# Output stores of a fused attention and feed-forward kernel: one transfer per chunk, or four of 32 rows

## The chip, the cores and the metric

The kernel runs on one core of a Trainium2 chip. The metric is the device time of one execution in microseconds; the kernel before takes 314.96 us (median of 3 runs, 313.32 to 315.15).

## What is computed

A Nystrom attention with 32 landmarks over 8 batches of 8 heads, 576 positions of width 64, and behind it a feed-forward layer with SiLU (512 to 2048 to 512) over all 4608 tokens:

```python
q_lm = q.reshape(B, H, m, S // m, D).mean(axis=3)     # m = 32, S // m = 18
k_lm = k.reshape(B, H, m, S // m, D).mean(axis=3)
A, Bm, C = sm(q, k_lm), sm(q_lm, k_lm), sm(q_lm, k)   # softmaxes
Z = Bm.transpose(0, 1, 3, 2) / (norm1 * norminf)
for _ in range(6):
    Z = 2 * Z - Z @ Bm @ Z
attn = A @ Z @ C @ v
h = x @ w_in                                          # x: attn as (4608, 512)
out = (h * sigmoid(h)) @ w_out                        # float32, (4608, 512)
```

## The kernel before

Work goes batch by batch (b = 0 to 7). A batch has three parts: attention (`attn(b)`), the first layer (`layer1(b)`: 16 blocks of 128 of the hidden width, `h` matmuls into PSUM, SiLU on ScalarE into `gm` and `gx`), and the second layer (`layer2_batch(b)`: four chunks of 128 tokens, in every odd batch a fifth for the rest of two batches; each chunk is 16 matmuls by `w_out_sb` in four pieces of four, a copy from PSUM to `ost`, and a store to the output). `ost` is a ring of 3 buffers. There are 36 chunks, so 36 stores of 256 KB.

The 576 positions of a batch are 32 groups l of 18 positions j, and the output row of a token is 18 l + j. A chunk's 128 rows are four values of j with 32 l each; its store (L881) is one transfer with the shape 4 x 32 x 512. The fifth chunk has rows (batch, l, j) with two values of j, and its store (L887) has the shape 64 x 2 x 512.

From batch 2 on, q, k and `ce` are transposed by DMA: four transposes give `qT` (L479), two give `ct` (L717), all issued by SyncE (SP), as are all stores. The loads of q, k and v come from GpSimd's queue (L368, L375). GpSimd also adds up the landmark means in a tree of six steps for k and six for q (L516), which ends in `lm`. Loads and transposes take turns: `ct` of batch b waits for the v loads of batch b+1, the `qT` transposes of batch b+1 wait for `ct` of batch b, and the loads of batch b+2 wait for the `qT` transposes of batch b+1.

TensorE needs `lm` for the landmark scores (through `lmT`, then `sb`), `qT` for `A` and `C`, and `ct` for the product with v (`cv`). After `cv` come `zt`, `m` and the first layer.

The order of work on each engine is fixed before the program is built. The class `Plan` simulates the engines with a cost for each operation (its time on the engine, a lag until others see its result, for some a time on a shared DMA line, `dma=`) and hands out the free operation of the highest priority. The instructions are then written in that order. The costs are numbers in the source; a change of a cost changes the order on all engines, and each engine works strictly in its order.

Of the kernel before, what the change touches and what calls it, by code (L numbers as in the profile page):

```python
# [254 lines left out]
def kernel(  # L255
# [9 lines left out]
    nc = tc.nc  # L265
# [11 lines left out]
    sc = 1.0 / float(Dh) ** 0.5  # L277
    SW = 128 + L
    NPE = 2
    XLAG = 0.7  # L280

    constp = ctx.enter_context(tc.tile_pool(name="constp", bufs=1))
    natp = ctx.enter_context(tc.tile_pool(name="natp", bufs=1))
# [6 lines left out]
    def bank(o, i=0):  # L290
        return banks[o.slot[i]]
# [142 lines left out]
    def attn(b):  # L434
# [12 lines left out]
        if on_pe:  # L447
            blocks = {}
            me["qk_read"] = []
            for t in (1, 0):  # L450
                todo = [(g, jp) for g in range(NG) for jp in range(JP)]
                for i in range(0, 18, 4):
                    part = todo[i:i + 4]

                    def tmm(e, t=t, part=part, key=(t, i)):
                        ps = bank(blocks[key])
                        for n, (g, jp) in enumerate(part):
                            mm(ps[:, n * 128:(n + 1) * 128],
                               qk[:, t, g, 2 * jp:2 * jp + 2, :].rearrange("p j d -> p (j d)"),
                               idb)  # L460
                    o = blocks[t, i] = A(f"tr{t}{i}.{b}", [("PE", mm_us(128, len(part)))], tmm,
                                         [qk_ops[b, t], cid], p0 + 7 + (1 - t) * 0.5, psum=1)
                    me["qk_read"].append(o)

                    def tcp(e, t=t, i=i, n=len(part), key=(t, i)):
                        copy(e, qT[:, t].rearrange("p g j x -> p (g j) x")[:, i:i + n, :],
                             bank(blocks[key])[:, 0:n * 128].rearrange("p (n x) -> p n x", x=128))
                    c = A(f"trc{t}{i}.{b}", either(128 * len(part)), tcp, [o], p0 + 8).reads(o)
                    for g, _ in part:
                        qt_ops.setdefault((t, g), []).append(c)  # L470
        else:
            me["qk_read"] = []
            me["xts"] = []
            gate = v_ops[b][-1:] if b == NPE else prev["cts"]
            for t in (1, 0):
                for g in range(NG):
                    qt_ops[t, g] = [A(
                        f"xt{t}{g}.{b}", [("SP", 0.1)],
                        lambda e, t=t, g=g: nc.sync.dma_start_transpose(  # L479
                            out=qT[:, t, g], in_=qk[:, t, g].rearrange("p j d -> p (j d)")),  # L480
                        [qk_ops[b, t]] + use + gate, p0 + 5, dma=1.42, lag=XLAG)]
                    qt_ops[t, g][0].after = gate
                    me["qk_read"] += qt_ops[t, g]
                    me["xts"] += qt_ops[t, g]
# [191 lines left out]
        for g in range(NG):  # L676
# [36 lines left out]
                            bank(me["ctm", g, i0])[:, 0:384]), [o, prev.get("cv")],  # L713
                        p0 + 20).reads(o))
            else:
                ct_ops[g] = [A(f"ct{g}.{b}", [("SP", 0.1)], lambda e, ce=ce, ct=ct:
                               nc.sync.dma_start_transpose(  # L717
                                   out=ct, in_=ce.rearrange("p i x -> p (i x)")),
                               xs + [prev.get("cv")] + v_ops.get(b + 1, [])[-1:], p0 + 20, dma=1.42, lag=XLAG)]
                ct_ops[g][0].after = v_ops.get(b + 1, [])[-1:]  # L720
                me["cts"] += ct_ops[g]

# [66 lines left out]
    def layer1(b):  # L789
# [5 lines left out]
        for dc in range(NDC):  # L795
# [19 lines left out]
            if dc % 8 == 7:  # L815
# [3 lines left out]
                def xm(e, d0=d0, cell=cell):  # L819
                    ps = bank(cell["o"]).rearrange("p (c x) -> p c x", c=8)  # L820
                    for d in range(8):
# [10 lines left out]
                gx_ops[b].append(A(  # L832
                    f"gx{d0}.{b}", [("ACT", act_us(512))],
                    lambda e, d0=d0, cell=cell, c=c: nc.scalar.activation(  # L834
                        out=gx[:, d0:d0 + 8, c:c + 64].rearrange("p d (l j) -> p d j l", j=2),
                        in_=bank(cell["o"]).rearrange("p (d j l) -> p d j l", d=8, j=2),
                        func=AF.Silu),
                    [o], p + 0.5, table="silu").reads(o))
                gx_ops[b][-1].unit = b
        l1_done[b] = A(f"l1done.{b}", [("SP", 0.0)], lambda e: None, pes, 0.0, lag=0.0)  # L840
# [5 lines left out]
    def layer2(src, deps, prio, stores, split=False):  # L846
# [3 lines left out]
        for qt in range(4):  # L850
# [8 lines left out]
            if qt == 0:  # L859
# [5 lines left out]
        ost = ost_r[i]  # L865
        c = A(f"oc@{prio}", either(512), lambda e: copy(e, ost, bank(head[0])),
              [prev_piece, ost_st.get(i)], 900.0 + prio / 100).reads(head[0])
        st = A(f"os@{prio}", [("SP", 0.15)], lambda e: stores(ost), [c], prio, dma=0.65, lag=1.6)
        ost_st[i] = st
        return pieces  # L870

    def rows(b, n):
        return out[b * S:(b + n) * S, :].rearrange("(b l j) n -> b j l n", b=n, j=J)

    def layer2_batch(b):
        l2_last["m", b] = []
        for c in range(4):
            j0 = 8 * (c % 2) + c // 2

            def stores(ost, j0=j0):  # L880
                return nc.sync.dma_start(out=rows(b, 1)[0, j0:j0 + 7:2], in_=ost)  # L881
            l2_last["m", b] += layer2(
                lambda dc, c=c: gm_r[b % 3][:, dc, c * 128:(c + 1) * 128], lambda qt: gm_ops[b][4 * qt:4 * qt + 4],
                5000.0 + 100 * b + 10 * c, stores)
        if b % 2 == 1:
            def stores(ost):
                return nc.sync.dma_start(  # L887
                    out=out[(b - 1) * S:(b + 1) * S, :].rearrange(
                        "(b l j) n -> b l j n", b=2, j=J)[:, :, J - 2:J].rearrange(
                            "b l j n -> b l (j n)"), in_=ost)  # L890
            l2_last["x", b // 2] = layer2(
                lambda dc: gx_r[(b // 2) % 2][:, dc, :], 
                lambda qt: [gx_ops[b - 1][qt // 2], gx_ops[b][qt // 2]],
# [16 lines left out]
    with tc.manual_schedule(engines={ET.PE, ET.Activation, ET.DVE, ET.Pool, ET.SP}):  # L910
        table = None
        for o, e, t, end, switch in order:
# [2 lines left out]
                    act_func_set_id=EXP_SET, name=nc.get_next_instruction_name(),  # L915
                    engine=ET.Activation))
            r = o.emit(e)
            if o.dma:
                o.ins = r.ins
            for x in o.after:  # L920
                tc.add_manual_dep(o.ins, x.ins.name, mybir.DependencyInfo(
                    mybir.DependencyClass.Sync, mybir.DependencyReason.DATA),
# [34 lines left out]
```

## Time and profile before

| | |
|---|---|
| time, median of 3 runs | 314.96 us |
| time of the profiled execution | 314.78 us |
| its span, first to last instruction | 313.0 us |
| mean granted TensorE clock | 0.937 of 2.4 GHz |
| TensorE matmul busy | 269.5 us (86%) |
| ScalarE busy | 179.7 us (57%) |
| GpSimd busy | 106.9 us (34%) |
| VectorE busy | 96.6 us (31%) |
| queue of GpSimd's loads | 18.35 MB, 35.3% of 16 DMA engines |
| queue of SP's stores and transposes | 18.88 MB, 29.6% of 16 DMA engines |

Busy shares are means over the span. A transfer counts on the DMA engines by the time that its packets took. SP does no computing; a row "SPq" is the time that SP took to issue a transfer, not the time that it needed to land.

### The profile page before, as it was taken

What the parts mean: (1) busy time and instruction counts of PE and PEld (TensorE: products, weight loads), DVE (VectorE), ACT (ScalarE), POOL (GpSimd) and SP (SyncE); (2) the same over time, 40 slices, a digit from 0 to 9 for tenths busy, and PEclk for the clock granted to TensorE, in tenths of its full rate; (3) what the DMA queues carried; (4) which work ended last, traced back from release to release, by engine and by line L of the source; (5) the groups of instructions that cost most, each with busy time, mean ns of one, the idle gap of its engine ahead of it and who ended that gap; (6) DMA issues with size and microseconds to landing.
All of it is one profiled execution on the core that took longest, in us unless ns stands there. A gap on an engine that the chain in (4) does not pass through costs nothing.

```text
span 313.0 us, 5933 instructions
## 1 busy us (share of the span) xinstructions
PE 269.5 (86%) x2367; PEld 135.0 (43%) x2367; DVE 96.6 (31%) x258; ACT 179.7 (57%) x405; POOL 106.9 (34%) x133
## 2 busy tenths in 40 slices
PE   7998999939889638998799249997999999999991
PEld 5965545414344214453444024444445544444440
DVE  1676028400555611405346114035365300000000
ACT  1776986448826914898149209985369975112110
POOL 8157319453924590485041931295000000000000
PEclk9999999968999956999799659999999999999998
DMA  6999997969386928696669257866951011132222
GB/s 113 209 197 201 206 209 129 163 136 169 60 135 123 206 66 178 116 154 69 129 132 199 68 71 139 165 98 106 193 95 44 17 31 37 40 96 64 75 68 97
DMA packets 58076, 37.60 MB, mean 120 GB/s; under 512 B 39105, under 2 KB 49345, under 8 KB 58049
## 3 DMA queue, kind: packets, MB, share of 16 engines
q0 software_dynamic: 15232, 18.35, 35.3%
q1 hardware_dynamic: 42816, 18.88, 29.6%
q8 instruction: 18, 0.29, 0.4%
q14 instruction: 10, 0.07, 0.1%
HBM read 36.70 MB, written 9.44 MB: 147 GB/s over the span
## 4 chain that ended last, share of the span: by engine, by line
PE 52%; DMA 29%; ACT 6%; POOL 4%; SPq 3%; issue 2%; DVE 2%; POOLq 0%; ACTq 0%
PE ps L323 52%; DMA v<-in_v_dram 11%; DMA ct<-ce 7%; DMA w_in_sb<-in_moe_w_in_dram 7%; SPq L479 3%; ACT gm L811 3%; DMA qT<-qk 3%; POOL qk L368 2%; POOL v L375 2%; ACT gx L834 1%; ACT L914 1%; DVE bbd L576 1%; ACT ce L691 0%; DVE bm L570 0%; POOL lm L516 0%
## 5 line engine op out<-in xcount | busy, mean ns | idle before, releaser
L323 PE MATMUL ps<-w_out_sb,gm 128*128 128x512 bf16 x512 | 122.1, 382 | 0.0
L811 ACT ACTIVATE gm<-ps 128x512 bf16<-128x512 f32 x128 | 67.4, 642 | 30.6 <-PE ps L323 30.4
L323 PE MATMUL ps<-etn,m 128*128 128x64 bf16 (+1 forms) x512 | 75.5, 299 | 0.1
L323 PEld LDWEIGHTS <-gm 128*128 128x128 bf16 x512 | 47.4, 98 | 52.7 <-issue 2.9
L323 PEld LDWEIGHTS <-m 128*128 128x128 bf16 x512 | 33.1, 101 | 30.1 <-issue 7.1
L333 ACT COPY ost<-ps 128x512 f32<-128x512 f32 x25 | 14.7, 587 | 50.8 <-PE ps L323 50.7
L516 POOL TENSOR_TENSOR sa<-qk 128x576 f32<-128x576 bf16 x24 | 31.0, 1311 | 34.4 <-DMA qk<-in_k_dram 33.9
L620 DVE SCALAR_TENSOR_TENSOR st<-st,ps 128x320 bf16<-128x320 bf16 (+3 forms) x54 | 21.6, 408 | 46.0 <-PE ps L323 42.8
L323 PE MATMUL ps<-v,ct 96*64 96x128 bf16 x192 | 10.0, 251 | 15.6 <-DMA ct<-ce 14.7
L368 POOL DMA_DIRECT2D qk<-in_k_dram x8 | 6.0, 745 | 51.2 <-DMA qT<-qk 50.0
L335 DVE CAST m<-ps 128x512 bf16<-128x512 f32 x31 | 19.8, 686 | 9.0 <-PE ps L323 9.0
L516 POOL TENSOR_TENSOR sb<-sa 128x512 f32<-128x512 f32 (+1 forms) x24 | 21.6, 901 | 1.8
L333 ACT CAST m<-ps 128x512 bf16<-128x512 f32 x33 | 17.9, 617 | 3.0 <-PE ps L323 2.9
L323 PE MATMUL ps<-idb,lm 128*128 128x128 bf16 x32 | 4.7, 240 | 16.5 <-POOL lm L516 16.5
L335 DVE COPY ost<-ps 128x512 f32<-128x512 f32 x11 | 7.6, 689 | 32.7 <-PE ps L323 32.7
L375 POOL DMA_DIRECT2D v<-in_v_dram x24 | 13.9, 589 | 6.1 <-DMA w_out_sb<-in_moe_w_out_dram 3.7
L323 PE MATMUL ps<-w_out_sb,gx 128*128 128x512 bf16 x64 | 15.9, 379 | 0.0
L323 PEld LDWEIGHTS <-ct 96*64 96x64 bf16 x192 | 7.1, 126 | 20.3 <-DMA ct<-ce 17.2
L323 PE MATMUL ps<-zer 128*128 128x256 bf16 x95 | 14.5, 295 | 1.1 <-DVE zer L402 1.1
L323 PE MATMUL ps<-st 128*128 128x160 bf16 (+1 forms) x96 | 15.2, 234 | 0.0
L691 ACT ACTIVATE ce<-ps 128x288 bf16<-128x288 f32 x32 | 12.7, 412 | 3.9 <-PE ps L323 3.9
L323 PEld LDWEIGHTS <-st 128*128 128x128 bf16 x96 | 9.3, 103 | 12.3 <-issue 3.7
(68 smaller groups left out, 260.7 us busy)
## 6 DMA issues: line engine op xcount, KB each, us to landing
out_dram<-ost SPq DMA_DIRECT2D x36, 256.0 KB
qk<-in_k_dram POOLq DMA_DIRECT2D x8, 576.0 KB, 9.4
qk<-in_q_dram POOLq DMA_DIRECT2D x8, 576.0 KB, 12.3
v<-in_v_dram POOLq DMA_DIRECT2D x24, 192.0 KB, 13.3
w_out_sb<-in_moe_w_out_dram POOLq DMA_DIRECT2D x4, 512.0 KB, 10.8
w_in_sb<-in_moe_w_in_dram POOLq DMA_DIRECT2D x4, 256.0 KB, 9.6
w_in_sb<-in_moe_w_in_dram POOLq DMA_DIRECT2D x8, 128.0 KB, 7.4
qT<-qk SPq DMA_TRANSPOSE x24
```

Source lines behind the costliest of these rows:

```text
L323: nc.tensor.matmul(out=out_ap, lhsT=lhsT, rhs=rhs, start=start, stop=stop, skip_group_check=True)
L333: nc.scalar.copy(out=out, in_=in_)
L335: nc.vector.tensor_copy(out=out, in_=in_)
L368: lambda e, t=t, src=src: nc.gpsimd.dma_start(out=qk_r[b % 2][:, t].rearrange("p g j d -> p g (j d)"), in_=src[b].rearrange("(g h) (l j) d ...
L375: lambda e, a=a: nc.gpsimd.dma_start(out=v_r[b % 2][a * L:(a + 1) * L, :, :], in_=v[b].rearrange("h (l a x) d -> a l h (x d)", l=L, a=VA)[ ...
L479: lambda e, t=t, g=g: nc.sync.dma_start_transpose(out=qT[:, t, g], in_=qk[:, t, g].rearrange("p j d -> p (j d)")),
L516: lambda e: nc.gpsimd.tensor_tensor(out=o_, in0=a_, in1=b_, op=OP.add),
L576: bbd_op = chain("bbd", 0.2, lambda: nc.vector.tensor_tensor(out=bbd, in0=bc(bmt, 4, 2), in1=bc(hmask, NG, 1), op=OP.mult), [bmt_op, prev. ...
L620: nc.vector.scalar_tensor_tensor(out=s2[:, g0:g1, lo:SW], in0=s[:, g0:g1, lo:SW], scalar=2.0, in1=ps[:, 0:NG * SW].rearrange("p (g x) -> p ...
L691: nc.scalar.activation(out=ce[:, :, 0:VP].rearrange("p (i c) (a l) -> p c a i l", c=2, a=VA)[:, c], in_=bank(me[f"C{g}"], c)[:, 0:HS].rear ...
L811: lambda e, dc=dc, cell=cell: nc.scalar.activation(out=gm[:, dc, :], in_=bank(cell["o"]), func=AF.Silu),
L834: lambda e, d0=d0, cell=cell, c=c: nc.scalar.activation(out=gx[:, d0:d0 + 8, c:c + 64].rearrange("p d (l j) -> p d j l", j=2), in_=bank(ce ...
```

## The change

Each store of a chunk is issued as four transfers, one for each j (32 rows of 512 numbers, 64 KB). For the fifth chunk to be cut in this way its rows must lie as (batch, j, l), so the SiLU of `gx` writes them as they come from PSUM and no longer interleaved. The planner's costs change too: a transpose takes 1.38 of SP (before 0.1, and 1.42 of the DMA line), a chunk's store 2.2 of SP (before 0.15, and 0.65 of the DMA line), the lag of a transpose is 1.9 (before 0.7), that of a store 1.9 (before 1.6). The last piece of the diff only keeps the instruction for the manual dependencies of operations that have no `dma` any more.

```diff
-    XLAG = 0.7
+    XLAG = 1.9
...
-                        f"xt{t}{g}.{b}", [("SP", 0.1)],
+                        f"xt{t}{g}.{b}", [("SP", 1.38)],
...
-                        [qk_ops[b, t]] + use + gate, p0 + 5, dma=1.42, lag=XLAG)]
+                        [qk_ops[b, t]] + use + gate, p0 + 5, lag=XLAG)]
...
-                ct_ops[g] = [A(f"ct{g}.{b}", [("SP", 0.1)], lambda e, ce=ce, ct=ct:
+                ct_ops[g] = [A(f"ct{g}.{b}", [("SP", 1.38)], lambda e, ce=ce, ct=ct:
...
-                               xs + [prev.get("cv")] + v_ops.get(b + 1, [])[-1:], p0 + 20, dma=1.42, lag=XLAG)]
+                               xs + [prev.get("cv")] + v_ops.get(b + 1, [])[-1:], p0 + 20, lag=XLAG)]
...
-                        out=gx[:, d0:d0 + 8, c:c + 64].rearrange("p d (l j) -> p d j l", j=2),
-                        in_=bank(cell["o"]).rearrange("p (d j l) -> p d j l", d=8, j=2),
-                        func=AF.Silu),
+                        out=gx[:, d0:d0 + 8, c:c + 64],
+                        in_=bank(cell["o"]).rearrange("p (c x) -> p c x", c=8), func=AF.Silu),
...
-        st = A(f"os@{prio}", [("SP", 0.15)], lambda e: stores(ost), [c], prio, dma=0.65, lag=1.6)
+        st = A(f"os@{prio}", [("SP", 2.2)], lambda e: stores(ost), [c], prio, lag=1.9)
...
-    def rows(b, n):
-        return out[b * S:(b + n) * S, :].rearrange("(b l j) n -> b j l n", b=n, j=J)
+    def store_js(b, js, ost, p0):
+        for i, j in enumerate(js):
+            nc.sync.dma_start(out=out[b * S:(b + 1) * S, :].rearrange("(l j) n -> j l n", j=J)[j],
+                              in_=ost[p0 + L * i:p0 + L * i + L, :])
...
-                return nc.sync.dma_start(out=rows(b, 1)[0, j0:j0 + 7:2], in_=ost)
+                store_js(b, range(j0, j0 + 7, 2), ost, 0)
...
-                return nc.sync.dma_start(
-                    out=out[(b - 1) * S:(b + 1) * S, :].rearrange(
-                        "(b l j) n -> b l j n", b=2, j=J)[:, :, J - 2:J].rearrange(
-                            "b l j n -> b l (j n)"), in_=ost)
+                for bb in range(2):
+                    store_js(b - 1 + bb, (J - 2, J - 1), ost, 64 * bb)
```

The order on GpSimd differs at one place, in batch 2: the end of the tree for `lm_88` (its steps into `sb_87` and `lm_88`) and the loads of batch 3 into `qk_81` and `v_85`. Minus is before, plus the changed kernel:

```order
 L516 TENSOR_TENSOR sa_86<-sb_87 128x2x128
+L516 TENSOR_TENSOR sb_87<-sa_86 128x2x64
+L516 TENSOR_TENSOR lm_88<-sb_87,sa_86 128x256
 L368 DMA qk_81<-in_k_dram 128x2x1152
 L368 DMA qk_81<-in_q_dram 128x2x1152
 L375 DMA v_85<-in_v_dram 32x8x384 x3
-L516 TENSOR_TENSOR sb_87<-sa_86 128x2x64
-L516 TENSOR_TENSOR lm_88<-sb_87,sa_86 128x256
 L516 TENSOR_TENSOR sa_86<-qk_81 128x576 x2
```

The two tree steps have moved ahead of the five loads. On SP, these are the transfers from the `qT` transposes of batch 3 (into `qT_83`) to the `ct` transposes of batch 4 in the kernel before:

```order
L479 DMA_TRANSPOSE qT_83<-qk_81 128x9x128 x4
L881 DMA out_dram<-ost_125 4x32x512
L881 DMA out_dram<-ost_123 4x32x512
L881 DMA out_dram<-ost_124 4x32x512
L717 DMA_TRANSPOSE ct_110<-ce_108 128x6x128
L717 DMA_TRANSPOSE ct_111<-ce_109 128x6x128
L887 DMA out_dram<-ost_125 64x2x512
L479 DMA_TRANSPOSE qT_82<-qk_80 128x9x128 x4
L881 DMA out_dram<-ost_123 4x32x512
L717 DMA_TRANSPOSE ct_110<-ce_108 128x6x128
```

and the same stretch in the changed kernel:

```order
L479 DMA_TRANSPOSE qT_83<-qk_81 128x9x128 x4
L873 DMA out_dram<-ost_125 32x512 x4
L873 DMA out_dram<-ost_123 32x512 x4
L873 DMA out_dram<-ost_124 32x512 x4
L873 DMA out_dram<-ost_125 32x512 x4
L717 DMA_TRANSPOSE ct_110<-ce_108 128x6x128
L717 DMA_TRANSPOSE ct_111<-ce_109 128x6x128
L479 DMA_TRANSPOSE qT_82<-qk_80 128x9x128 x4
L873 DMA out_dram<-ost_123 32x512 x4
L717 DMA_TRANSPOSE ct_110<-ce_108 128x6x128
```

Each store is four rows, and the store of the fifth chunk stands before the `ct` transposes of batch 3 and no longer behind them. Between the `qT` and the `ct` transposes of batches 2 to 6 there were 2, 3, 1, 4 and 2 stores, and there are 2, 4, 1, 4 and 2 now. On TensorE the order is the same up to batch 2 and differs from there on in where the second layer's pieces stand.

## Rows read from the trace of the kernel before

**Rows 1.** The chain that ended last, by engine, shares of the span (page).
```profile
PE 52%; DMA 29%; ACT 6%; POOL 4%; SPq 3%; issue 2%; DVE 2%; POOLq 0%; ACTq 0%
```

**Rows 2.** Windows: stretch, us; busy (count) PE PEld DVE ACT POOL; clock, DMA share, GB/s.
```profile
60.00:244.00 184.00, 150.96 (x1411) 70.77 (x1407) 66.78 (x174) 116.49 (x268) 75.08 (x87) 0.90 0.69 125
184.00:192.00 8.00, 7.90 (x72) 4.15 (x73) 1.84 (x7) 4.44 (x9) 0.00 (x0) 0.72 0.89 145
246.00:306.00 60.00, 60.00 (x321) 27.80 (x319) 1.30 (x3) 21.18 (x40) 0.00 (x0) 1.00 0.19 54
```

**Rows 3.** Timeline of TensorE: start, us, instruction, [idle before <-what ended it].
```profile
68.88 0.39 PE L323 MATMUL ps<-idb,lm 128*128 128x128 bf16 x2 [5.37 <-POOL lm L516]
...
111.75 0.40 PE L323 MATMUL ps<-idb,lm 128*128 128x128 bf16 x2 [4.96 <-POOL lm L516]
...
118.38 0.85 PE L323 MATMUL ps<-v,ct 96*64 96x128 bf16 x12 [4.26 <-DMA ct<-ce]
...
150.33 0.53 PE L323 MATMUL ps<-v,ct 96*64 96x128 bf16 x12 [2.50 <-DMA ct<-ce]
...
176.96 0.40 PE L323 MATMUL ps<-idb,lm 128*128 128x128 bf16 x2 [4.21 <-POOL lm L516]
...
184.10 0.85 PE L323 MATMUL ps<-v,ct 96*64 96x128 bf16 x12 [5.89 <-DMA ct<-ce]
```

**Rows 4.** Timeline of GpSimd around the loads of batch 3.
```profile
57.80 0.72 POOL L516 TENSOR_TENSOR sa<-sb 128x256 f32<-128x256 f32 x1
64.38 0.73 POOL L368 DMA_DIRECT2D qk<-in_k_dram  x1 [5.85 <-DMA qT<-qk]
...
68.10 0.72 POOL L516 TENSOR_TENSOR lm<-sb,sa 128x256 bf16<-128x256 f32 x1
```

**Rows 5.** Chain that ended last, in order of time: start, us, what.
```profile
92.89 3.73 DMA qT<-qk
...
99.78 15.76 DMA v<-in_v_dram
...
115.59 2.75 DMA ct<-ce
...
145.36 5.50 DMA ct<-ce
```

**Rows 6.** Timeline of SP: issues of a store and of two groups of transposes.
```profile
84.52 0.54 SPq L881 DMA_DIRECT2D out_dram<-ost  x1
86.16 8.20 SPq L479 DMA_TRANSPOSE qT<-qk  x4
...
119.81 5.58 SPq L479 DMA_TRANSPOSE qT<-qk  x4
```

**Rows 7.** Line L375 (v loads), windows 128:132, 64:68, 97:101, 159:163 in turn.
```profile
DMA to landing us min/median/max: 8.9/9.3/9.8
...
DMA to landing us min/median/max: 13.0/13.3/13.7
...
DMA to landing us min/median/max: 13.4/15.3/15.8
...
DMA to landing us min/median/max: 17.0/19.0/19.6
```

**Rows 8.** Windows on stores: two stretches of an L881 store, one of an L887 store.
```profile
255.00:256.00 1.00, 1.00 (x6) 0.49 (x5) 0.00 (x0) 1.00 (x3) 0.00 (x0) 1.00 0.21 10
...
257.00:258.00 1.00, 1.00 (x6) 0.46 (x5) 0.00 (x0) 1.00 (x4) 0.00 (x0) 1.00 0.26 100
...
119.40:120.30 0.90, 0.90 (x3) 0.30 (x2) 0.00 (x0) 0.06 (x1) 0.00 (x0) 0.50 0.79 291
```

**Rows 9.** Line L881: duration of an issue on SP, ns min/median/max, first and last start.
```profile
L881 SPq DMA_DIRECT2D out_dram<-ost x32: 535/537/711, 47.3 to 303.7; - x32
```

**Rows 10.** Groups of instructions from 244 to 307 us: count, busy us, mean ns.
```profile
L323 PE MATMUL ps<-w_out_sb,gm 128*128 128x512 bf16 x200 | 44.5, 379 | 0.0
```

**Rows 11.** Timeline of the end: the last store.
```profile
307.14 0.57 SPq L887 DMA_DIRECT2D out_dram<-ost  x1
```

More of the change, by code (lines that the diff above doesn't have):

```diff
@@ L917 @@
             r = o.emit(e)
-            if o.dma:
-                o.ins = r.ins
+            o.ins = getattr(r, "ins", None)
             for x in o.after:
```

## The prediction

> **What bounds the kernel now.** The chain of work that ended last is half TensorE and 29% DMA [rows 1]. I read first where the DMA part sits. The busy times by stretch [rows 2] show two regimes: from 246 to 306 us TensorE is busy without a gap at the full 2.4 GHz, working off the second layer, which needs nothing but finished tiles. From 60 to 244 us it is busy for 151.0 of 184.0 us, so it idles for 33.0, with a mean granted clock of 0.90. After a stall it is still slow: 0.72 from 184 to 192 us while busy almost throughout. So the first thing to find is what it waits for between 60 and 244 us.
>
> The timeline of TensorE names the six largest stalls, 27.2 us together [rows 3]: three for `lm` (the means from GpSimd), three for `ct` (a DMA transpose). All hang on one loop of transfers, one turn per batch b from 2 on, in which kinds of transfers take turns: the four `qT` transposes of b land; GpSimd issues the q, k and v loads of b+1; the last v load lands; the two `ct` transposes of b go out and land; then the `qT` transposes of b+1. The chain shows one turn [rows 5]: the last `qT` transpose of batch 3 starts at 92.89 and lands 3.73 later, the last v load takes 15.76, the `ct` transposes 2.75, and then TensorE goes on at 118.38 [rows 3].
>
> Why does a v load take that long? The four v rows [rows 7] are the same loads after different numbers of output stores on SP between the `qT` and the `ct` transposes: with none in the way (128 to 132 us) the median is 9.3 us, with two 13.3, with three 15.3, with four 19.0. That is (19.0 - 9.3)/4 = 2.4 us for each store. The shares of the DMA engines tell why [rows 8]. A store of L881 in steady flow (257 to 258 us) uses a share of 0.26 and moves 100 GB/s: about 4 of the 16 engines. The one store form whose outermost count is 64 and not 4 (L887, 119.4 to 120.3 us) uses 0.79 and moves its 256 KB in 0.9 us at 291 GB/s. A load is done when its slowest engine is done, so a store that keeps 4 engines busy for 2.6 us (256 KB at 100 GB/s) holds it up that long.
>
> The same shows in the transposes [rows 6]: four `qT` transposes take 5.58 us of SP after an L887 store, 8.20 us after an L881 store. And `ct` of batch 4, whose chain piece is 5.50 us instead of 2.75 [rows 5], goes out just behind an L881 store.
>
> **The change part by part.**
>
> *The stores.* Each of 36 becomes four transfers of 32 rows, outermost count 32. No row has this very form. If it spreads as the form with 64 rows does, a chunk costs a load 0.9 us. The bounds: 0.7 (0.9 times the share of 0.79) below; above, 2.4 (nothing gained) or, if each of the four has a start of its own, more (second rival). I take 0.9, since the form is nearest to L887's: rows outermost. The Trainium skill ("DMA: Bandwidth & Descriptors", section "Why a DMA increments its semaphore by 16 and not by 1") says that a transfer runs on the largest number up to 16 that divides the outermost counts of both sides: 4 for the old form, 16 for 32 rows. The shares of 0.26 and 0.79 agree; that 32 rows get 16 too no row here shows.
>
> *Issue.* One issue takes 0.54 us of SP [rows 9], for 128 rows. I take the same for 32 rows: 2.15 us per chunk, 1.6 more. It matters only where transposes stand behind a store. In the new order that is before the `qT` transposes of batches 2, 3, 6 and 7. At the last three the store runs while `ct` lands (2.75 us from the start of the second `ct` issue; with 5.58/4 = 1.4 us for that issue, 1.4 + 2.15 - 2.75 = 0.8 late each); at batch 2 the 1.6 counts in full. Together 4.0 us of the loop, against 2.6 (8.20 - 5.58) won at each place where an old store was in front. No store in the new order stands before a transpose while its copy needs that transpose, so SP does not block itself.
>
> *Order on GpSimd.* The last two tree steps of batch 2 now stand before the loads of batch 3. Today they wait with these loads for the `qT` transposes: GpSimd is done at 58.52, idles 5.85 us, issues five loads and gives `lm` only at 68.82 [rows 4]. In the new order `lm` is there two steps after 58.52, at 0.8 us each at most by 60.1 us, before TensorE asks for it at 68.88 - 5.37 = 63.5. The stall of 5.37 us goes.
>
> *Order on TensorE.* From batch 2 on the planner, told of longer transposes and stores, puts more second-layer pieces before the waits. After the last `sb` of the program the order has 272 matmuls by `w_out_sb` in the kernel before and 240 in the changed one: 8 pieces of four fewer, at 44.5/200 x 4 = 0.89 us each [rows 10]. This is no work saved; it fills stalls. The contiguous write of `gx` I cost at nothing: 16 instructions on ScalarE, which is not the bound there.
>
> *What is left of the stalls.* Batch 3 now has four stores in its turn where it had three: its v load goes from 15.3 to 9.3 + 4 x 0.9 = 12.9, 2.4 us less, and of the stalls 4.96 + 4.26 some 6.8 stay. Batch 5 has four in both: 19.0 becomes 12.9, 6.1 less, and of 4.21 + 5.89 some 4.0 stay. Batch 4's 2.50 goes, since its `ct` lands 2.75 us sooner. For all smaller stalls I leave 1. So idle time goes from 33.0 to about 12: -21.
>
> *Clock.* At a lower clock the busy time between 60 and 244 us is stretched: by at least 7.90 x 0.28 = 2.2 us in one 8 us window, by at most 151.0 x 0.10 = 15.1. I take 8 and let it shrink with the idle time (12/33): -5.
>
> *End.* After the last copy there are now four issues instead of one, the last 1.6 us later, but 64 KB on all engines behind no 4-engine store; today it is 313.0 - 307.14 = 5.9 us from issue to end [rows 11]. Between -1 and +1.6; I take 0.
>
> Sum: 313.0 - 21 - 5 = 287. The profiled execution's time was 1.8 us over its span (314.78 to 313.0), and 0.2 under the median of 314.96. So 289 us.
>
> **The rivals.**
>
> *Nothing gained per chunk* (price stays 2.4). Then the loop does not shrink: TensorE saves 5.4 us at `lm` and waits as much longer at the next `ct`; batch 3's turn grows by one store (2.4), the issues add 4.0, the pieces moved forward give 8 x 0.89 = 7.1 back: -0.7, about 314. For it speaks that no row shows this form; against it that both forms seen behave as their outermost count.
>
> *Four starts instead of one: slower.* In the first stretch of an L881 store (255 to 256 us) a share of 0.21 moves 10 GB/s [rows 8]: its engines are held for about 1 us while almost nothing moves. If each small transfer did this on all 16 engines, a chunk would cost 4 x 1.0 + 0.7 = 4.7 us. The turns of batches 2, 3 and 5 have 2 + 4 + 4 chunks for 2 + 3 + 4: 10 x 4.7 - 9 x 2.4 = 25.4, plus 4.0 of issue, less 7.1: +22, about 337. It decides from 10 p = 21.6 + 7.1 - 4.0, p = 2.5 us per chunk, 0.62 per transfer. Against it: the L887 store has its 256 KB through in 0.9 us. The Trainium skill (same page, "Rules for kernel authors") advises against this change: coalesce small transfers, as under 64 KB one pays mostly overhead, and don't split over partitions. These are of 64 KB; whether the overhead holds the engines or only delays the landing is what decides, and only the second is harmless here.
>
> *The order misfires.* The loop shrinks, but the order, made for other delays, has new stalls, in front of `C` of batches 3 and 5 above all, where more pieces now come first. Half of the gain: about 302.
>
> **How the numbers follow.** Forecast 0.72, nothing gained 0.12, four starts 0.08, misfire 0.08. The likeliest case alone spans 281 (price 0.7: -1.6; clock loss of 15: -4.5; end and small stalls: -1 each) to 299 (the stalls of both turns as now: +8.5, and 2 of clock with them). The range must also take in the misfire and reach towards the first rival above, and below the case that one of the two stalls left goes too: 278 to 309. A measurement of this kernel tells 1% from no change, 3.1 us. Faster: forecast, misfire and a little of the first rival, 0.82; same 0.10; slower 0.08.
>
> **What would show it.** SP: groups of four issues near 0.54 us; `qT` transposes of batches 2, 3 and 7 at about 5.6 us for four. Medians of the v loads at 13 us or less with four chunks in the turn; about 15 or more there proves me wrong on the price. Windows with stores alone: shares well over 0.26. No stall for `lm` near 64 us; stalls of 7 and 4 us at batches 3 and 5; second layer from about 225 us on without gaps. If the stalls for `ct` stay as they are, the first rival holds.

## The result, and the profile after

The changed kernel takes 283.8 us (median of 4 runs, 283.38 to 284.51) where the kernel before took 314.4 us beside it: a ratio of 0.903, with a 95% interval of 0.900 to 0.907. The prediction was 289 us with a range of 278 to 309. The span of the profiled execution fell from 313.0 to 282.8 us, and the mean granted clock rose from 0.937 to 0.981.

The windows of the changed kernel, with the columns of [rows 2]:

```profile
60.00:244.00 184.00, 171.26 (x1548) 80.99 (x1573) 66.65 (x173) 132.23 (x305) 74.78 (x85) 0.97 0.68 127
104.00:112.00 8.00, 6.13 (x53) 3.04 (x51) 0.89 (x3) 3.36 (x7) 5.18 (x6) 0.57 0.64 122
257.00:258.50 1.50, 1.50 (x8) 0.68 (x7) 0.00 (x0) 0.58 (x1) 0.00 (x0) 1.00 0.53 135
250.00:278.00 28.00, 27.66 (x127) 12.28 (x126) 0.00 (x0) 4.83 (x9) 0.00 (x0) 1.00 0.30 76
```

The forecast's sign for the spread is there: with stores alone, from 257 to 258.5 us, the DMA share is 0.53 where [rows 8] show 0.26 (third row).

From 60 to 244 us TensorE idles for 12.7 us, where [rows 2] give 33.0. The low clock has not gone: from 104 to 112 us it is 0.57 of 2.4 GHz, near the 1.2 GHz level, but there is less of it.

This accounts for the span, 30.2 us shorter. Idle time between 60 and 244 us: 33.0 to 12.7, so 20.3 less. Busy time of TensorE over the whole span: 269.5 to 262.5, so 7.0 less for the same work; this is what the clock gave back (32 of the 2367 matmul records are missing after, so it may be a little less, and the idle time with it). Idle time before 60 us: 1.5 less. Idle time from 244 us to the end: 1.4 less.

The stalls of TensorE that answer to [rows 3], from its timeline in the changed kernel:

```profile
103.50 0.28 PE L323 MATMUL ps<-idb,lm 128*128 128x128 bf16 x2 [1.02 <-POOL lm L516]
106.57 0.85 PE L323 MATMUL ps<-v,ct 96*64 96x128 bf16 x12 [1.87 <-DMA ct<-ce]
...
159.72 0.28 PE L323 MATMUL ps<-idb,lm 128*128 128x128 bf16 x2 [2.18 <-POOL lm L516]
...
162.52 0.53 PE L323 MATMUL ps<-v,ct 96*64 96x128 bf16 x12 [0.75 <-DMA ct<-ce]
```

The six stalls of [rows 3] made 27.2 us. No stall between 60 and 244 us is over 2.2 us now, and the two turns with four stores keep 2.9 us each (1.02 + 1.87 and 2.18 + 0.75).

The v loads, line L375, answering to [rows 7]: windows 61:65 (two stores in the turn), 90:94 (four), 116:120 (none), 145:149 (four), in this order:

```profile
DMA to landing us min/median/max: 9.4/9.8/10.2
...
DMA to landing us min/median/max: 10.1/10.6/11.0
...
DMA to landing us min/median/max: 8.7/9.1/9.5
...
DMA to landing us min/median/max: 11.0/11.3/11.8
```

A chunk of the turn costs a load (10.6 - 9.1)/4 to (11.3 - 9.1)/4, so 0.4 to 0.55 us. It was 2.0 to 2.4 [rows 7]: (13.3 - 9.3)/2 and (15.3 - 9.3)/3 give 2.0, and the 2.4 of the prediction is the figure from four stores.

Not all sixteen transfers of a turn run beside the loads. The time to landing of the stores (line L873), windows 86:90.9 and 91.5:98 (the turn of batch 3), then 142.9:145.8 and 145.85:153 (the turn of batch 5):

```profile
DMA to landing us min/median/max: 1.7/1.8/3.6
...
DMA to landing us min/median/max: 4.9/5.7/6.7
...
DMA to landing us min/median/max: 1.7/1.7/2.0
...
DMA to landing us min/median/max: 4.7/6.0/6.5
```

In the first turn eight transfers landed early and eight late, in the second six and ten. If only the late ones hold the loads up, 256 KB beside the loads cost (10.6 - 9.1)/2 to (11.3 - 9.1)/2.5, so an estimated 0.75 to 0.9 us. The turn with two chunks does not fit this count (two late transfers for 9.8 - 9.1 = 0.7 us), so it stays an estimate.

SP in the changed kernel: first the line of the stores (issue on SP, ns min/median/max, then the time to landing), then groups of its timeline, answering to [rows 6, 9]:

```profile
L873 SPq DMA_DIRECT2D out_dram<-ost x144: 314/422/1704, 46.2 to 279.9; - x144
...
DMA to landing us min/median/max: 1.6/1.7/6.7
```

```profile
52.52 6.55 SPq L479 DMA_TRANSPOSE qT<-qk  x4
...
75.65 2.54 SPq L717 DMA_TRANSPOSE ct<-ce  x2
78.29 1.92 SPq L873 DMA_DIRECT2D out_dram<-ost  x4
80.37 5.66 SPq L479 DMA_TRANSPOSE qT<-qk  x4
...
103.79 2.54 SPq L717 DMA_TRANSPOSE ct<-ce  x2
107.95 5.61 SPq L479 DMA_TRANSPOSE qT<-qk  x4
...
159.74 2.54 SPq L717 DMA_TRANSPOSE ct<-ce  x2
162.38 3.21 SPq L873 DMA_DIRECT2D out_dram<-ost  x4
165.75 5.67 SPq L479 DMA_TRANSPOSE qT<-qk  x4
```

From batch 3 on four `qT` transposes behind stores take about 5.7 us now, where [rows 6] show 8.20; those of batch 2, at 52.52, still take 6.55. The `ct` transposes that went out at 115.59 [rows 5] go out at 103.79.

The chain that ended last, against [rows 1]:

```profile
PE 55%; DMA 17%; POOL 10%; ACT 8%; SPq 4%; issue 3%; another core or an unknown queue 1%; POOLq 0%; DVE 0%; ACTq 0%
```

The DMA part fell from 29% to 17%. The rest is spread over engines that take turns.

### The profile page after: what moved, and what is told of

It reads as the page before. It is cut to its first block, busy times and chain, and to the rows that moved or that the text cites. A ratio compares the mean times of both kernels' runs of the same rounds, so it can differ in the third digit from the quotient of the medians.

```text
span 282.8 us, 6072 instructions
## 1 busy us (share of the span) xinstructions
PE 262.5 (93%) x2335; PEld 132.5 (47%) x2367; DVE 94.2 (33%) x253; ACT 178.4 (63%) x410; POOL 107.6 (38%) x133
## 4 chain that ended last, share of the span: by engine, by line
PE 55%; DMA 17%; POOL 10%; ACT 8%; SPq 4%; issue 3%; another core or an unknown queue 1%; POOLq 0%; DVE 0%; ACTq 0%
PE ps L323 55%; DMA w_in_sb<-in_moe_w_in_dram 7%; DMA qk<-in_k_dram 5%; POOL sa L516 5%; POOL sb L516 3%; SPq L479 3%; ACT gm L811 2%; DMA qT<-qk 2%; DMA ct<-ce 2%; ACT L811 1%; POOL lm L516 1%; POOL qk L368 1%; SPq L873 1%; ACT ce L691 1%
## 5 line engine op out<-in xcount | busy, mean ns | idle before, releaser
L323 PE MATMUL ps<-w_out_sb,gm 128*128 128x512 bf16 x482 | 117.1, 379 | 2.4 <-issue 1.3
L323 PE MATMUL ps<-etn,m 128*128 128x64 bf16 (+1 forms) x512 | 71.6, 292 | 0.6 <-ACT gm L811 0.6
L811 ACT ACTIVATE gm<-ps 128x512 bf16<-128x512 f32 x128 | 66.6, 647 | 6.1 <-PE ps L323 6.0
L333 ACT COPY ost<-ps 128x512 f32<-128x512 f32 x28 | 16.4, 587 | 55.4 <-PE ps L323 43.4
L323 PE MATMUL ps<-zer 128*128 128x256 bf16 x95 | 15.3, 307 | 1.1 <-DVE zer L402 1.1
L375 POOL DMA_DIRECT2D v<-in_v_dram x24 | 14.0, 590 | 6.2 <-DMA w_out_sb<-in_moe_w_out_dram 3.8
L691 ACT ACTIVATE ce<-ps 128x288 bf16<-128x288 f32 x32 | 12.7, 410 | 5.6 <-PE ps L323 5.6
L335 DVE COPY ost<-ps 128x512 f32<-128x512 f32 x8 | 5.5, 688 | 26.7 <-PE ps L323 26.7
L667 DVE TENSOR_TENSOR etn<-et,ln 128x576 bf16<-128x576 bf16 x16 | 13.4, 837 | 2.5 <-ACT ln L662 2.5
L648 ACT ACTIVATE et<-ps 128x288 bf16<-128x288 f32 x32 | 11.4, 416 | 3.5 <-PE ps L323 3.3
L323 PEld LDWEIGHTS <-st 128*128 128x128 bf16 x96 | 8.4, 99 | 10.7 <-issue 1.8
L323 PE MATMUL ps<-w_in_sb,zt 64*32 64x512 bf16 x256 | 11.6, 382 | 0.8 <-DMA w_in_sb<-in_moe_w_in_dram 0.4
```

Of the source, the lines that this page charges most:

```text
L323: nc.tensor.matmul(out=out_ap, lhsT=lhsT, rhs=rhs, start=start, stop=stop, skip_group_check=True)
L333: nc.scalar.copy(out=out, in_=in_)
L335: nc.vector.tensor_copy(out=out, in_=in_)
L375: lambda e, a=a: nc.gpsimd.dma_start(out=v_r[b % 2][a * L:(a + 1) * L, :, :], in_=v[b].rearrange("h (l a x) d -> a l h (x d)", l=L, a=VA)[ ...
L648: lambda e, g=g, et=et, c=c: nc.scalar.activation(out=et[:, c], in_=bank(me[f"A{g}"], c)[:, 0:HS], func=AF.Exp, scale=sc / J),
L667: nc.vector.tensor_tensor(out=etn[:, g, :], in0=et.rearrange("p c x -> p (c x)"), in1=ln.rearrange("p c x -> p (c x)"), op=OP.mult)
```

## Experiments

The theory: the gain comes from the stores no longer holding four engines, so that loads and transposes land earlier; the new order adds a smaller part of its own. The rivals: it is the order; it is the size or the number of the transfers. In all runs the kernel before was timed beside the new ones, with medians of 315.2 to 315.5 us.

### The order alone, and the stores alone

The first kernel has the planner's new costs, and so the order of the changed kernel, but one transfer of 4 x 32 x 512 for each chunk. The second has the four transfers, but the old costs and the old order.

```diff
 # the order alone: the kernel before with
-    XLAG = 0.7
+    XLAG = 1.9
...
-        st = A(f"os@{prio}", [("SP", 0.15)], lambda e: stores(ost), [c], prio, dma=0.65, lag=1.6)
+        st = A(f"os@{prio}", [("SP", 2.2)], lambda e: stores(ost), [c], prio, lag=1.9)
```

```diff
 # the stores alone: the changed kernel with
-    XLAG = 1.9
+    XLAG = 0.7
...
-        st = A(f"os@{prio}", [("SP", 2.2)], lambda e: stores(ost), [c], prio, lag=1.9)
+        st = A(f"os@{prio}", [("SP", 0.15)], lambda e: stores(ost), [c], prio, dma=0.65, lag=1.6)
```

> The new order alone: the planner's costs of the change, but each chunk still stored by one transfer of 4 x 32 x 512. Theory (the spread of a store over the DMA engines shortens the loop of transfers, the order fills what is left): a store still costs the v loads 2.4 us each, v loads of batches 4 and 6 beside four stores at a median of about 19 us, the stall for lm in batch 2 gone but given back at the next ct; about 312 us (305 to 318). Rival (the order alone did it, the form of the stores is beside the point): about 284 us.

> The new stores alone: four transfers of 32 rows each, with the planner's old costs and so the old order. Theory: v loads at a median of 11 us or less, qT transposes at 5.6 us for four; left are the lm stall of batch 2 (5.4 us) and 8 second-layer pieces that come late (7.1 us): 284 plus at most 12.5, so 288 to 297 us. Rival (the order alone did it): about 314 us.

The order alone: 309.4 us (308.4 to 311.2), ratio 0.983 (0.976 to 0.991). The stores alone: 293.6 us (293.1 to 294.3), ratio 0.933 (0.926 to 0.941). The windows from 60 to 244 us, first of the order alone, then of the stores alone:

```profile
60.00:244.00 184.00, 157.40 (x1433) 71.88 (x1423) 69.27 (x171) 118.97 (x277) 74.33 (x85) 0.93 0.70 126
```

```profile
60.00:244.00 184.00, 167.62 (x1533) 79.42 (x1533) 69.59 (x178) 130.37 (x298) 75.26 (x87) 0.94 0.69 125
```

TensorE idles for 26.6 and 16.4 us there (33.0 before, 12.7 with both). The stores are worth 21.5 us by themselves and the order 5.8. Together they are worth 31.4 by the 283.8 us above, or 29.6 by a repeat of the changed kernel that was timed beside these two (285.6 us, further below), so the order gives 8.0 to 9.8 on top of the stores. With the old order and the new stores the largest stalls are those for `lm`, on TensorE's timeline:

```profile
65.82 0.39 PE L323 MATMUL ps<-idb,lm 128*128 128x128 bf16 x2 [3.38 <-POOL lm L516]
...
107.54 0.39 PE L323 MATMUL ps<-idb,lm 128*128 128x128 bf16 x2 [5.18 <-POOL lm L516]
```

Of these the changed kernel keeps 1.02 us at 103.50. Both times came out as the theory expected. One expectation did not: with the order alone, the v loads of batch 6 (line L375, window 157:161) took 19.7 us beside four stores, but those of batch 4 (window 94:99) only 15.4:

```profile
DMA to landing us min/median/max: 17.8/19.7/20.5
...
DMA to landing us min/median/max: 15.1/15.4/15.8
```

The difference speaks for the theory. One of the four stores in the turn of batch 3 is the fifth chunk's, in the old form with 64 outermost rows, and the loads landed as early as beside three stores before (15.3 [rows 7]).

### One large transfer that spreads

If the outermost count is what matters, one transfer of 256 KB with 32 outermost does as well as four of 64 KB. VectorE writes the attention weights in the order (l, j), so that the chunk's rows lie as the output wants them; that takes three instructions where there was one. The order is that of the kernel before.

```diff
-                nc.vector.tensor_tensor(out=etn[:, g, :], ...)
+                for c in range(2):
+                    nc.vector.tensor_tensor(
+                        out=ev[:, c, 0:256].rearrange("p (u l j) -> p u j l", u=2, j=4), ...)
+                nc.vector.tensor_tensor(out=ev[:, :, 256:288], ...)
...
-                return nc.sync.dma_start(out=rows(b, 1)[0, j0:j0 + 7:2], in_=ost)
+                return nc.sync.dma_start(out=out[b * S:(b + 1) * S, :].rearrange(
+                    "(l j) n -> l j n", j=J)[:, j0:j0 + 7:2], in_=ost)
```

> One transfer per chunk, but of shape 32 x 4 x 512 (outermost count 32): VectorE writes the columns of etn in the order (l, j), at three instructions in place of one, so that a chunk's rows lie as (l, j). Old costs, old order. Theory (spread, not number): like the four new transfers in the old order, 288 to 297 us, v loads at 11 us or less. Rival (the cut into small transfers counts): about 314 us.

289.5 us (288.7 to 291.2), ratio 0.920 (0.913 to 0.927). The windows and the stores' time to landing (line L884):

```profile
60.00:244.00 184.00, 171.23 (x1598) 80.71 (x1596) 82.86 (x207) 132.97 (x302) 75.61 (x87) 0.98 0.64 125
252.00:254.00 2.00, 2.00 (x11) 0.87 (x9) 0.00 (x0) 0.50 (x1) 0.00 (x0) 1.00 0.49 183
...
DMA to landing us min/median/max: 2.4/2.5/8.7
```

One transfer of the old size with 32 outermost brings TensorE's idle time down to 12.8 us too. Cutting into small transfers is not needed for the gain; the spread is. This kernel even beats the stores alone by 4 us with the same planner costs, though VectorE is busy for 82.9 us in this stretch where it was 66.8 in the kernel before.

### Two transfers per chunk: half the engines

> The changed kernel with two transfers per chunk, each of two j (2 x 32 x 512, 128 KB), everything else as in the changed kernel. Theory (the outermost count sets the number of engines): two engines, at the 25 GB/s each of the old form (100 GB/s on 4), so 128 KB take 2.6 us; a share of about 0.13 in a stretch with stores alone; per chunk 2.6 us (if the second transfer takes other engines than the first) to 5.2 us (if both take the same), so nothing is gained on the old form or up to 2.8 us lost per chunk: 307 to 340 us, against 309.4 for the same order with one transfer of 4 x 32 x 512. Rival (smaller transfers, or the other order of stores, made the gain): between the changed kernel's 283.8 and 297 us, share above 0.3.

```diff
-        for i, j in enumerate(js):
-            nc.sync.dma_start(out=...rearrange("(l j) n -> j l n", j=J)[j],
-                              in_=ost[p0 + L * i:p0 + L * i + L, :])
+        for i in range(0, len(js), 2):
+            nc.sync.dma_start(out=...rearrange("(l j) n -> j l n", j=J)[js[i]:js[i] + d + 1:d],
+                              in_=ost[p0 + L * i:p0 + L * i + 2 * L, :])
```

(`d` is the step from one j to the next.) 379.2 us (378.1 to 380.2), ratio 1.205 (1.199 to 1.210). One window, a stretch with stores alone, and one row of what waited for what in this kernel (us in total, times, longest us). The last line is of its v loads after two chunks (line L375, window 64:72):

```profile
316.00:318.00 2.00, 2.00 (x11) 0.92 (x10) 0.00 (x0) 0.58 (x1) 0.00 (x0) 1.00 0.13 51
```

```profile
ACT ost L333 <- DMA out_dram<-ost: 48.6, 11, 11.0
```

```profile
DMA to landing us min/median/max: 16.0/17.9/18.9
```

A share of 0.13 at 51 GB/s is two engines of 16 at 25 GB/s each, as the theory had it, and both transfers of a chunk together use no more: 256 KB take 5.1 us per chunk. The v loads agree: 17.9 us after two chunks and 9.1 in the turn with none (window 145:154), so 4.4 us per chunk, where four engines cost 2.0 to 2.4. The time is far above the 307 to 340 us that I expected, because I had priced only the loop of transfers. There is a second bound: the copies to `ost` wait for stores that have not landed. Seven of the eleven waits, 27.7 us, come after 317 us, where the second layer runs at the pace of the stores. The direction is clear: fewer outermost rows, fewer engines, a slower kernel, and this with smaller transfers than before.

An edit that was to give the four small transfers only four engines each (the 32 rows written as 4 x 8) was misjudged: the two dimensions lie one behind the other in memory and merge again, so the built program had the same transfers as the changed kernel.

```diff
-                ...rearrange("(l j) n -> j l n", j=J)[j],
+                ...rearrange("(a l j) n -> j a l n", a=4, j=J)[j],
```

> As the changed kernel, order included, but each of the four transfers is written as 4 x 8 x 512 (outermost count 4) in place of 32 x 512. Theory (what counts is on how many DMA engines a store runs): as bad as one transfer of 4 x 32 x 512, v loads beside four chunks near 19 us, about 312 us (305 to 320). Rival (what counts is that a store is cut into four small transfers): about 284 us.

285.6 us (283.9 to 286.3), ratio 0.906. It is a repeat of the changed kernel and says nothing on the engines. It does show how far the price per chunk varies from one execution to the next: its v loads in the turns with four, none and four chunks (line L375, windows 90:95, 116:121 and 145:150) give (10.5 - 9.2)/4 to (12.2 - 9.2)/4, so 0.3 to 0.75 us.

```profile
DMA to landing us min/median/max: 10.1/10.5/10.8
...
DMA to landing us min/median/max: 8.8/9.2/9.6
...
DMA to landing us min/median/max: 11.8/12.2/12.6
```

### One large transfer with the new order, and what VectorE costs

The one-transfer kernel with the planner's new costs should have come near the changed kernel.

> The changed kernel's order and planner costs, but each chunk's store is one transfer of 32 x 4 x 512, with VectorE writing the weights' tile in the order (l, j) in three instructions instead of one; the fifth chunk is stored as before (64 x 2 x 512). Theory (what counts is over how many engines a store spreads, and beside it the order): the order was worth 5.8 us with the old store (315.2 to 309.4) and 9.8 us with four transfers (293.6 to 283.8), so it takes some 4 to 9 us off the 289.5 us of one transfer with the old order: 280 to 286, the same as the changed kernel within 1%. v loads at 8 to 11 us in all turns. Rival (four transfers are worth something by themselves, since loads and transposes get in between them): it stays at 288 to 292, v loads of 12 us or more in the turns with four stores.

289.5 us (286.6 to 291.0), ratio 0.917 (0.913 to 0.922): not the theory's number but the rival's. Yet its v loads land in 8.6 to 14.2 us with a median of 10.6, nearly the same as in the changed kernel. The time is lost in one place: the turn from the `qT` to the `ct` transposes of batch 2. They go out at 53.25 and 82.20 us there, and at 52.52 and 75.65 us in the changed kernel, so this turn is 5.8 us longer. TensorE has new stalls for VectorE, the first of 3.21 us for `st` at 58.14. That could be the price of the three instructions. So the same three instructions went into the changed kernel, with four transfers:

```diff
+                for c in range(2):
+                    nc.vector.tensor_tensor(
+                        out=ev[:, c, 0:256].rearrange("p (u l j) -> p u j l", u=2, j=4),
+                        in0=et[:, c, 0:256].rearrange("p (u l j) -> p u j l", u=2, j=4), ...)
...
```

> The changed kernel, four transfers per chunk, order as in the changed kernel, and only the multiplication into etn on VectorE is cut into the three instructions per group that the one-transfer kernels have (strided access, same result). It carries their VectorE cost (some 14 us more busy on VectorE) without their store. Theory (what holds one transfer with the changed order at 289.5 us above the changed kernel's 283.8 us is VectorE, whose matrix steps come late: the turn of batch 2 from the qT to the ct transposes took 28.9 us there and 23.1 us in the changed kernel): this one rises to 287 to 292 us, with stalls of TensorE behind VectorE near 58 and 110 us and the first turn at 27 us or more. Rival (four transfers are better by themselves, since loads get in between them): it stays at 283 to 286 us.

291.0 us (290.3 to 291.7), ratio 0.924 (0.920 to 0.928). First TensorE's timeline of this kernel, then the line of the instruction with its ns min/median/max, here and in the one-transfer kernel:

```profile
58.10 0.37 PE L323 MATMUL ps<-idb,lm 128*128 128x128 bf16 x2 [3.40 <-DVE st L620]
...
108.48 0.31 PE L323 MATMUL ps<-st 128*128 128x160 bf16 x2 [2.26 <-DVE st L620]
112.52 0.23 PE L323 MATMUL ps<-st 128*128 128x32 bf16 x2 [2.64 <-DVE st L620]
```

```profile
L669 DVE TENSOR_TENSOR etn<-et,ln x32: 718/776/1818, 27.3 to 220.8; 128x256 bf16<-128x256 bf16 x32
```

```profile
L669 DVE TENSOR_TENSOR etn<-et,ln x32: 707/782/1724, 27.5 to 220.6; 128x256 bf16<-128x256 bf16 x32
```

The cost of this instruction is the same in both (776 and 782 ns), and the times, 291.0 and 289.5 us, are half a per cent apart with ratios whose intervals overlap. So one or four transfers make no difference that counts in this order, and the 4 to 7 us above the changed kernel (283.8, and 285.6 in the repeat) are VectorE's: in this order the matrix steps `st` have no slack. With the old order one transfer was faster than four in spite of this cost (289.5 against 293.6 us); what makes up for it there no run separates.

### Eight transfers per chunk

> The changed kernel with each chunk stored as eight transfers of 16 rows (32 KB) instead of four of 32; all else the same. Theory (a transfer costs the loads what its bytes take on all engines, and little for its start, so the number of transfers matters by SP's issue alone): with 0.42 us an issue a chunk takes SP 3.4 us instead of 1.7; where stores stand right before transposes (about four places in the loop) that is up to 1.7 us each: 284 to 292 us, v loads still 8 to 12 us. Rival (each start holds the engines, which four transfers just do not show yet): v loads in turns with four chunks at 14 us or more and 300 us or more.

```diff
-            nc.sync.dma_start(out=...[j], in_=ost[p0 + L * i:p0 + L * i + L, :])
+            for h in range(0, L, 16):
+                nc.sync.dma_start(out=...[j, h:h + 16],
+                                  in_=ost[p0 + L * i + h:p0 + L * i + h + 16, :])
```

307.5 us (303.7 to 308.9), ratio 0.972 (0.965 to 0.979). Neither number: the time is the rival's, the mechanism is not. The v loads with four chunks in the turn (windows 90:99 and 149:156 of L375) and SP's timeline in the first of these turns:

```profile
DMA to landing us min/median/max: 9.2/10.1/10.6
...
DMA to landing us min/median/max: 10.6/11.3/12.0
```

```profile
83.56 6.49 SPq L479 DMA_TRANSPOSE qT<-qk  x4
90.15 19.31 SPq L874 DMA_DIRECT2D out_dram<-ost  x32
109.57 2.56 SPq L717 DMA_TRANSPOSE ct<-ce  x2
```

The loads land as early as in the changed kernel (10.1 and 11.3 us for 10.6 and 11.3). By their landing times 13 and 17 of the 32 transfers (416 and 544 KB) ran beside the loads, where the changed kernel has 8 and 10 late ones (512 and 640 KB), so more starts cost the loads nothing that shows. SP is the bound: 32 issues fill it for 19.3 us, the `ct` transposes stand behind them, and they go out only when the last issue is done (109.57; 103.79 in the changed kernel, whose turn began 3.2 us earlier). The estimate of 0.42 us an issue gave 32 x 0.42 = 13.4 us, or 14.7 with the 0.46 from one issue to the next; the rest is time in which SP waited between issues, for the copies and for earlier stores to land. The turn of batch 5 looks the same (32 issues from 149.56, 19.27 us, `ct` at 168.95).

That is not the whole loss. Against the changed kernel the `ct` transposes are 5.8 us late at batch 3, 9.2 at batch 5 and 17.8 at batch 7, and the end 24.4. In the turns of batches 3 and 5 ScalarE's copies to `ost` waited 4.26 and 5.80 us for stores, and TensorE then 3.60 and 5.60 us for ScalarE (at 100.29 and 161.25). At the end, where only the second layer is left, a chunk takes SP 8 x 0.46 = 3.7 us (from one issue to the next) and the copies come every 3.5 us, so SP falls behind: its issues last until 304.8 us, where the last copy is done at 295.9. From the last copy to the end of the span it takes 11.3 us here, and 4.4 in the changed kernel. SP's timeline (window 275:308) and ScalarE's:

```profile
274.89 29.89 SPq L874 DMA_DIRECT2D out_dram<-ost  x64
...
295.31 0.58 ACT L333 COPY ost<-ps 128x512 f32<-128x512 f32 x1 [1.92 <-DMA out_dram<-ost]
```

### The tree step alone

The prediction counts a stall of 5.37 us for `lm` of batch 2 in full. Here only GpSimd's order changes: the five loads of batch 3 go behind the last two tree steps of batch 2.

```diff
     order = P.run()
+    late = [qk_ops[3, 1], qk_ops[3, 0]] + v_ops[3]
+    moved = [r for r in order if r[0] in late]
+    order = [r for r in order if r[0] not in late]
+    at = [r[0].name for r in order].index("le0.2") + 1
+    order[at:at] = moved
```

> The kernel before with one thing moved: the five loads of batch 3 on GpSimd stand behind the last two steps of the landmark tree of batch 2. All other engines keep their order. Theory (most of that stall is given back): lm of batch 2 is there by 61 us and the stall of 5.37 us at 68.88 goes, but the loop of transfers gains only what its ct transposes (issued at 81.88, behind ce) can go out earlier until the v loads hold them, which land near 80 us: about 2 us, so 312 to 314 us. Rival (the stall counts in full, as the prediction's sum has it): 309 to 310.5 us.

313.5 us (310.4 to 316.0), ratio 0.993 (0.989 to 0.996), as the theory said. GpSimd's and then TensorE's timeline:

```profile
58.47 0.72 POOL L516 TENSOR_TENSOR lm<-sb,sa 128x256 bf16<-128x256 f32 x1
63.32 0.73 POOL L368 DMA_DIRECT2D qk<-in_k_dram  x1 [4.13 <-DMA qT<-qk]
```

```profile
79.99 0.39 PE L323 MATMUL ps<-idb,lm 128*128 128x128 bf16 x2 [3.04 <-POOL lm L516]
86.53 0.28 PE L323 MATMUL ps<-idb,lm 128*128 128x128 bf16 x2 [1.73 <-POOL lm L516]
...
116.75 0.85 PE L323 MATMUL ps<-v,ct 96*64 96x128 bf16 x12 [6.48 <-DMA ct<-ce]
```

`lm` is there at 59.2 us and the stall at 68.88 [rows 3] is gone, but TensorE waits 3.04 and 1.73 us for the next `lm`, and its wait for `ct` in the next turn is 6.48 us where it was 4.26. The `ct` transposes of batch 2 go out at 79.44 instead of 81.88 us; of those 2.4 us, 1.9 reach the end. So here the stall of TensorE counted only as far as the loop of transfers got shorter by it.

## Why the prediction was right, point by point

**The cause** was right: stores on four engines held the loads up. It is shown from three sides: with 32 outermost in one transfer or in four the gain is there, with 2 outermost the kernel is slower, and the order without the stores gives 5.8 of some 30 us. The price per chunk follows the outermost count: 4.4 us with 2, 2.0 to 2.4 with 4, 0.3 to 0.75 with 32. The Trainium skill ("DMA: Bandwidth & Descriptors", section "Why a DMA increments its semaphore by 16 and not by 1") has the largest number up to 16 that divides both outermost counts. It agrees: 0.26 for 4 [rows 8], 0.13 for 2.

**The price per chunk** was somewhat too high: 0.9 us forecast, 0.7 as the lower bound, 0.4 to 0.55 measured, 0.3 to 0.75 in the repeat. The sum took it that all four chunks of a turn run beside the loads. In the changed kernel six to eight of their sixteen transfers had landed early; for the bytes that did run beside the loads the estimate above is 0.75 to 0.9.

**The issue** was right in kind: 0.42 us (median) instead of 0.54. Where a store stands between `ct` and `qT` it made the transposes about 1.9 us late from `ct` of batch 5 to `qT` of batch 6 (159.74 to 165.75 against 103.79 to 107.95 without a store, so 6.01 against 4.16) where 0.8 was forecast: one of the four issues took 1.70 us. From `ct` of batch 2 to `qT` of batch 3 the same distance is 80.37 - 75.65 = 4.7 us, so 0.6 late (it had been 86.16 - 81.88 = 4.3 us). That SP's issue has a price of its own the eight transfers showed.

**The `qT` transposes** came out as forecast from batch 3 on, 5.66 us for 5.6; those of batch 2 took 6.55.

**The order on GpSimd**: the stall went, as forecast, but the reason to count all 5.37 us was wrong; alone it is worth 1.9 us. **The order on TensorE**: with the old price per chunk the first rival's sum, without the issues of four transfers, would have been 314 - 4 = 310, and the order alone gave 309.4. That agreement is partly luck, as the sum has 2.4 us for a fourth store of batch 3's turn, which in its old form with 64 rows cost nothing there. With the new price the order is worth more, 8.0 to 9.8 us.

**The stalls left** came to 12.7 us for a forecast of 12, but of other parts: 2.9 and 2.9 us in the two turns for which I had 6.8 and 4.0, and 6.9 us of small ones for which I had 1. The lower price per chunk explains part of the first: with 0.5 instead of 0.9 a turn with four stores is 1.6 us shorter. The new order explains more. The sum had no term for the 8 second-layer pieces (7.1 us) that the order moves ahead of the waits, though both rivals' sums have one; with the old order the stores alone leave 5.18 + 1.46 and 2.02 + 2.20 us in these two turns, with three and four chunks in them (TensorE before 107.54, 111.36, 163.91 and 166.82), 10.9 where the changed kernel keeps 5.8 and the sum had 10.8. So the sum was right partly because two errors cancelled: too much left in two turns, too little in the small stalls.

**The clock** gave back up to 7.0 us, forecast 5; the bounds were 2.2 and 15.1. **The end** gave 1.4 us, where I took 0 with -1 as its bound: from the last matmul on nothing but 64 KB transfers is left to land. Against the 287 us of the sum the span of 282.8 us lacks 4.2: 2.0 by the clock, 1.4 by the end, 1.5 before 60 us, less 0.7 more of idle time after it. What came before 60 us is hardly the change: from 0 to 44 us TensorE was busy for 40.4 us in the kernel before, 42.2 after, and 41.6 to 42.7 in three experiments (the order alone, the stores alone, the tree step).

**The rivals.** Nothing gained per chunk falls with the v loads. Four starts falls with them, and more sharply with eight transfers, whose loads land no later. That rival agrees with the advice in the Trainium skill ("DMA: Bandwidth & Descriptors", section "Rules for kernel authors") to coalesce transfers: for this store the measurement decides against it, since 64 KB transfers on many engines did better than 256 KB on four. One 256 KB transfer on many engines did about as well, so coalescing was harmless here where the spread stayed. The order did not misfire, though it has lost its slack on VectorE, as the three instructions showed.

## What to carry to other kernels

Look at the DMA share of a stretch with one kind of transfer alone. A share near 4/16 or 2/16 went here with an outermost count of 4 or 2, whatever the size, and such stores delayed loads and transposes that were spread over all engines. Write the store so that its outermost dimension is long (32 and 64 rows did here); whether as one transfer or four is decided by what it costs the issuing queue (here 0.42 us each) and the engines that have to prepare the layout. The number of issues counts too: eight per chunk lost most of the gain. A stall of TensorE is not a gain in waiting: follow the loop that sets the pace, and count only what shortens it.

## What I had not expected of the hardware

- The time to landing of a 64 KB store is 1.7 us in the median but 4.7 to 6.7 us while loads run. ScalarE did not wait for it there: its five waits at the ring of `ost` (10.1 us in all, at most 2.0) come from 242 us on, when the loads are over and TensorE is busy for 27.66 of 28.00 us.
- Two transfers of a chunk issued one behind the other on two engines each kept within the share of two: 0.13 of 16 engines and 51 GB/s for both together.
- An issue on SP is not constant: 0.31 to 1.70 us for the same 64 KB transfer. What makes single ones long is left open.
- The start of a small transfer took nothing measurable from the loads: with 32 transfers of 32 KB in the turn (13 and 17 of them beside the loads) the v loads landed in 10.1 and 11.3 us, with 16 of 64 KB (8 and 10 beside them) in 10.6 and 11.3.
